# Eight plain float32 heads, three low-v splits on VectorE, and constants set up earlier in an attention and expert kernel

## The chip, the core and the metric

The kernel runs on one core of a Trainium2 chip. A core has TensorE (PE, with its weight loads shown as PEld), VectorE (DVE), ScalarE (ACT), GpSimd (POOL) and SyncE (SP), which issues most DMAs. The metric is the device time of one execution in microseconds (us), as a median of several runs.

## What is computed

Causal attention over 4 batches of 12 heads (448 positions, 64 columns per head), whose output is the input of a mixture of 8 experts: each of the 1792 positions goes to its best expert.

```
scores = scale * np.matmul(q, k.transpose(0, 1, 3, 2))     # masked above the diagonal
attn = exp(scores - max); attn = attn / (attn.sum(-1) + 1e-09)
x = attn @ v                                               # to [1792, 768]
logits = x @ w_gate + modality_bias[modality_id]
e_idx = argmax(logits);  gate_w = softmax(logits)[e_idx]
out[mask_e] = gate_w * (relu(x[mask_e] @ w1[e]) @ w2[e])   # for each expert e
```

## The kernel before

Products in full float32 take two passes of TensorE, each slow. So the kernel cuts most operands in a high part (rounded to the format fp32r) and a low part (the rest), and adds up products of parts in single passes. `hl` holds such parts of a pair of heads, `vhl` those of v for a group of four heads, `ph` and `pl` those of the transposed probabilities.

The attention stage is a loop of 48 iterations, `iteration(n)`, one per head, written out in software-pipeline order: TensorE in iteration n makes the scores of head n (`st_scores`, L270), transposes the probabilities of head n-2 (`st_trans`, L302), multiplies those of head n-3 with v (`st_pv`, L334 and L341, into the one bank `ot`), and from iteration 7 on joins heads and forms logits (`st_comb`, L394). VectorE takes the score maxima (L280, with accumulator reads), forms `pl` (L321), adds high and low halves of the output to `ut` (`st_out`, L365, which frees `ot`), and normalizes (L412, L422). ScalarE does the exponentials (L290), `ph` (L320) and the copy `hol` (L359).

GpSimd prepares operands ahead. For a pair m of heads, `split_qk(m)` (L194, L195) cuts query and key in iteration 2m-4, SP's `stack_qk(m)` (L211, L212) copies the parts into `st` in iteration 2m-3, and `split_kl(m)` (L200 the low key, L202 the zero-padded queries `qz`) follows there. For a group, `load_v`, `split_vh` (L242) and `split_vl` (L247) make `vhl`, of which there are two buffers. GpSimd also does every fourth normalization, parts of the routing (`route`), scatters (L501) and, at the end of attention, splits of the first expert's weights (`w1_chunk`, L675, L676).

The first pairs of heads skip all that: `first_load(m)` brings them in and `st_scores` multiplies them as plain float32 (`qh is None`). Before, these are the pairs 0 to 2, heads 0 to 5. The queries stand zero-padded in pieces of the raw buffers `raw1`, given by `first_view`.

Work that belongs to no head is put at an iteration with `later(n, f)`, `before(n, f)` or `soon(n, f)`, and `run_todo` runs it there: `setup_0`, `setup_1` and `setup_4` make constants, index tables and the modality bias, `shift_slots` (six pieces) makes slot constants, `after_batch` spreads the routing of a batch. The order of each engine's line is the order of this code; nothing is moved afterwards, and an engine waits at an instruction whose operands are not there.

After the loop the last heads are finished beside the first products of the experts (`pre_g1(t, ks)`: weight blocks ks of token block t), then comes the routing of the last batch (`choose`, `places` with products L476 to L482 on TensorE), then the experts.

Of the kernel before, what the change touches and what calls it, by code (L numbers as in the profile page):

```python
# [8 lines left out]
F32 = mybir.dt.float32  # L9
# [4 lines left out]
ALU = mybir.AluOpType  # L14
# [7 lines left out]
def attention_moe(  # L22
# [12 lines left out]
    V = nc.vector  # L35
    P = nc.gpsimd
    A = nc.scalar
    B, HP, _, _, S = qk.shape
# [3 lines left out]
    E, _, DF = w1.shape  # L42
# [3 lines left out]
    GH = 4  # L46
# [121 lines left out]
    def stack_view(t):  # L168
        return t[:, 0:2 * S].rearrange("p (c s) -> p c s", c=2)
# [15 lines left out]

    def load_qk(m):
        b, j = divmod(m, H // 2)
        raw[m] = t = stack_view(raw1[(5, 3, 4)[m % 3]])
        nc.sync.dma_start(out=t, in_=qk[b, j])

    def split_qk(m):
# [27 lines left out]
        stk.append([t[:, a] for a in range(2)])  # L219

    def first_view(m, c):
        k, j = (((3, 0), (3, 1), (4, 0)), ((2, 0), (2, 1), (4, 1)), ((0, 0), (0, 1), (1, 0)))[m][c]
        return raw1[k][:, j * S:(j + 1) * S]

    def first_load(m):
# [6 lines left out]
    def load_v(gr):  # L232
        b, u = divmod(gr, NG)
        c = slice(u * GH * D, (u + 1) * GH * D)
        nc.sync.dma_start(out=vraw[:, 0:3, :], in_=v[b, 0:384, c].rearrange("(t p) c -> p t c", p=128))
        nc.sync.dma_start(out=vraw[0:64, 3, :], in_=v[b, 384:448, c])
# [3 lines left out]
    def split_vh(gr):  # L240
        t = T([128, NTL, GH, 2, D], F32R, "vhl", 2)
        P.tensor_scalar(out=t[:, :, :, 0], in0=vsrc, scalar1=1.0, scalar2=0.0, op0=ALU.mult, op1=ALU.add)  # L242
        vhl[gr] = t

    def split_vl(gr):
        t = vhl[gr]
        P.tensor_tensor(out=t[:, :, :, 1], in0=vsrc, in1=t[:, :, :, 0].bitcast(F32), op=ALU.subtract)  # L247

    SPOS = [(0, 448), (1, 0), (1, 192), (0, 0)]
    ORD = (3, 0, 1, 2)  # L250
# [295 lines left out]
    def shift_slots(s, j):  # L546
        a = by_shift[s]
        if j == 0:
            ts(a[:, 0:1], tcol, 1.0, -float(s))
            ts(a[:, 1:2], tcol, 0.0, float(PZ - s))  # L550
            ts(a[:, 2:3], a[:, 0:1], float(2 * BLK), 0.0)
            ts(a[:, 3:4], a[:, 0:1], float(HB), 0.0)
        else:
            x = sm([128, 1], "slot")
            ts(x, a[:, 0:1], *((128.0, 128.0 * (PZ - s)) if j == 1 else (64.0, 192.0 * (PZ - s) + 128.0)))
            P.tensor_scalar(out=a[:, 2:3], in0=a[:, 2:3], scalar1=x, scalar2=0.0, op0=ALU.min, op1=ALU.add)
            if s and j == 2:
                P.tensor_tensor(out=a, in0=a, in1=by_shift[0], op=ALU.subtract)
# [318 lines left out]
    with tc.manual_schedule():  # L877
# [1 line left out]
            first_load(m)  # L879
        load_v(0)  # L880
        first_load(2)
        load_qk(3)
        nc.sync.dma_start(out=modi, in_=mod)
        nc.sync.dma_start(
            out=bias_sb.rearrange("p m o e -> p (m o e)"),
# [2 lines left out]

        V.memset(ones, 1.0)
        warm_bank = bank("x")  # L890
        for _ in range(24):
            nc.tensor.matmul(warm_bank[:, 0:128], lhsT=ones, rhs=ones, start=True, stop=True)
        warm = sm([1, 1], "warm")
        V.memset(warm, 0.0)
# [17 lines left out]
        for s in range(3):  # L912
            eng = P if s else V
            eng.memset(praw[s][0], 0.0)
            eng.memset(praw[s][1][:, 192:256], 0.0)
            eng.memset(praw[s][2][:, 320:384], 0.0)
            eng.memset(praw[s][3][:, 448:512], 0.0)
        wg = w_gate.rearrange("(j a p) e -> a p j e", a=2, p=64)
        for a in range(2):
            r = slice(a * 64, a * 64 + 64)  # L920
# [32 lines left out]
        def later(n, f):  # L953
            todo.setdefault(n, []).append(f)
# [9 lines left out]
                f()  # L964

        for j in range(2):
            later(3 + j, lambda j=j: V.memset(xg[j], 0.0))
            later(1 + j, lambda j=j: V.memset(sls[j][64:128, 0, E:E + 1], 1.0e6))
            later(1 + j, lambda j=j: V.memset(lts[j][64:128, 0], 0.0))

# [23 lines left out]

        later(0, setup_0)
        later(1, setup_1)
        later(2, lambda: V.memset(e8v[64:128, 0], 0.0))

        def setup_4():
            P.iota(ent[:, :, 0, 0], pattern=[[S, B]], base=0, channel_multiplier=1)  # L1000
# [55 lines left out]
        def pre_g1(t, ks):  # L1056
            if t not in g1b:
                g1b[t] = two_banks() if t else [bank("sa"), bank("sb")]
            for k in ks:
                for half in range(2):  # L1060
                    g1(t, half, g1b[t][half], [k])
# [12 lines left out]

        for k in range(KA):
            later(NHEAD - KA + k, lambda k=k: w1_chunk(k, P))
        later(4, setup_4)
        for s in range(2):
            for j in range(3):
                later(6 + 3 * s + j, lambda s=s, j=j: shift_slots(s, j))  # L1080

        def iteration(n):
            if n % 2 == 1 and 5 < n + 3 < NHEAD:
                stack_qk((n + 3) // 2)
            if n == 1:
                load_v(1)
            if n and n % GH == 0 and n // GH + 1 < B * NG:
                load_v(n // GH + 1)
            gr, i = divmod(n - 2 * GH, GH)
            comb = 0 <= gr < B * NG  # L1090
            if 0 <= n - 4 < NHEAD:
                st_out(n - 4)
            if comb:
                st_move(gr, i)
                st_norm(gr, i)
                b, u = divmod(gr, NG)
                if u == NG - 1:
                    later(n + 1, lambda i=i: x_store(b, i))
                    if i == NTL - 1:
                        after_batch(b, n)  # L1100
            run_todo((n,))
            if n in (2, 3):
                st_trans(n - 2)
            if n < NHEAD:
                st_scores(n)
            run_todo(n)
            if n == 0:
                split_vh(0)
                split_vl(0)
            if n % 2 == 1 and 5 < n + 3 < NHEAD:  # L1110
                split_kl((n + 3) // 2)
            if n % 2 == 0 and 5 < n + 4 < NHEAD:
                split_qk((n + 4) // 2)
            if n % GH == 1 and n > GH:
                st_sums(n // GH - 1, P)
            if n % GH == RECAT and n > GH:
                st_rec(n // GH - 1)
            if 0 <= n - 1 < NHEAD:
                st_exp(n - 1)
            if 0 <= n - 2 < NHEAD:  # L1120
                if n > 3:
                    st_trans(n - 2)
                run_todo(-n)
                st_split(n - 2)
            if 0 <= n - 3 < NHEAD:
                st_pv(n - 3)
                st_low(n - 3)
            gr, i = divmod(n - 2 * GH + 1, GH)
            if 0 <= gr < B * NG:
                st_comb(gr, i)  # L1130
            if n % GH == 2 and n // GH + 1 < B * NG:
                split_vh(n // GH + 1)
                split_vl(n // GH + 1)
            if n in (1, 3):
                load_qk(4 + n // 2)
            if n % 2 == 0 and n > 3 and n + 8 < NHEAD:
                load_qk((n + 8) // 2)

        for n in range(NHEAD):
            iteration(n)  # L1140
# [111 lines left out]
        for _, f in choose:  # L1252
            f()
        pre_g1(0, (3, 4))
        places()
        pre_g1(1, (0, 1, 2, 3))
        for i in range(2):
# [7 lines left out]
        sc_ = schedule_a(counts(B - 1))  # L1265
        for i in range(NTL):
            x_store(B - 1, i)
        pre_g1(0, (5,))
        ha, hb = (relu(o, i) for i, o in enumerate(g1b[0]))
        w2_chunk(2)  # L1270
        pre_g1(1, (4,))
# [154 lines left out]
```

## Time and profile before

| | |
|---|---|
| time, median of 3 runs | 499.09 us (496.9 to 499.83) |
| profiled execution: whole run, span of the trace | 498.88 us, 496.8 us |
| mean granted clock of TensorE, as a share of 2.4 GHz | 0.987 |
| busy: TensorE, VectorE, ScalarE, GpSimd | 470.7, 290.3, 276.4, 245.8 us |
| instructions | 10248 |

How to read it: an engine's row has the start in the span, the duration, the engine and line (of the kernel before), operation, out<-in, shapes and a count. In brackets stands the idle time of that engine just before, and after the arrow what ended it. Adjacent durations on an engine overlap a little, since instructions are pipelined; the distance from start to start is the cost. "x2" on a float32 product are its two passes.

### The profile page before, as it was taken

The numbers are of one execution on the slowest core, as the hardware profiler recorded it, in microseconds if no ns is written. First come the engines' busy times: TensorE is split into PE (matmuls) and PEld (weight loads), VectorE is DVE, ScalarE is ACT, GpSimd is POOL, SyncE is SP. The second block draws the span as 40 slices with busy tenths as digits, with TensorE's granted clock in tenths as the row PEclk, the third lists the DMA queues.
The fourth block names the chain that finished last, engine by engine and source line by source line (L and its number), as shares of the span: only waits on it lengthen the run. The fifth ranks groups of instructions, "written<-read, shape, count | busy, mean of one in ns | idle before, by whom it ended". The sixth has DMA issues, their size and how long they took to land. (4 is left out here: it accounts for less than half of the span.)

```text
span 496.8 us, 10248 instructions
## 1 busy us (share of the span) xinstructions
PE 470.7 (95%) x3307; PEld 443.0 (89%) x3307; DVE 290.3 (58%) x858; ACT 276.4 (56%) x680; POOL 245.8 (49%) x332
## 2 busy tenths in 40 slices
PE   8999899999899979989999999999999999999990
PEld 6799899999798979869999999999999999889770
DVE  4899899999889988987422017431120120283490
ACT  5799899999788978326212116612220211383670
POOL 8999999999999999942301104102001001021131
PEclk9999999999899999989999999999999999999997
DMA  7797799998987889491596204853001001076200
GB/s 189 199 257 214 183 236 251 281 237 206 292 214 182 188 182 327 126 202 3 163 381 208 81 1 144 292 203 98 34 1 53 33 2 63 33 279 194 104 13 7
DMA packets 43816, 78.91 MB, mean 159 GB/s; under 512 B 15582, under 2 KB 27614, under 8 KB 43744
## 3 DMA queue, kind: packets, MB, share of 16 engines
q1 hardware_dynamic: 40624, 66.94, 49.2%
q0 software_dynamic: 3040, 11.03, 6.6%
q8 instruction: 28, 0.46, 0.5%
q14 instruction: 44, 0.36, 0.3%
q10 hardware_dynamic: 80, 0.11, 0.1%
HBM read 48.10 MB, written 11.89 MB: 121 GB/s over the span
## 5 line engine op out<-in xcount | busy, mean ns | idle before, releaser
L732 POOL DMA_INDIRECT xg<-xs,idg x18 | 21.0, 1164 | 156.6 <-DVEq L1336 80.8
L290 ACT ACTIVATE p<-p,nm 128x448 f32<-128x448 f32 x192 | 94.8, 498 | 2.5 <-DVE nm L280 2.5
L770 DVE SCALAR_TENSOR_TENSOR htl<-g,hth 128x256 fp32r<-128x256 f32 x40 | 16.7, 425 | 104.6 <-ACT hth L769 104.6
L751 PE MATMUL g<-xh,w1h 128*128 128x256 f32 x240 | 67.1, 280 | 0.4 <-DVE htl L770 0.4
L753 PE MATMUL g<-xh,w1l 128*128 128x256 f32 x240 | 67.3, 280 | 0.0
L752 PE MATMUL g<-xl,w1h 128*128 128x256 f32 x240 | 67.0, 279 | 0.0
L321 DVE TENSOR_TENSOR pl<-pt,ph 128x1024 fp32r<-128x1024 f32 x48 | 58.3, 1215 | 7.6 <-ACT ph L320 7.2
L302 PE MATMUL pt<-ident,p 128*128 128x128 f32 x480 | 60.2, 273 | 0.0
L302 PEld LDWEIGHTS pt<-ident,p 128*128 128x128 f32 x480 | 55.3, 141 | 1.1
L334 PE MATMUL ot<-ph,vhl 128*128 128x448 f32 x192 | 50.5, 303 | 5.9 <-DVE ut L365 5.9
L320 ACT ACTIVATE ph<-pt 128x1024 fp32r<-128x1024 f32 x48 | 49.1, 1023 | 7.4 <-PE pt L302 6.3
L769 ACT ACTIVATE hth<-g 128x256 fp32r<-128x256 f32 x40 | 15.1, 383 | 63.5 <-PE g L753 63.5
L751 PEld LDWEIGHTS g<-xh,w1h 128*128 128x128 f32 x240 | 44.9, 187 | 0.6 <-DVE htl L770 0.6
L811 POOL DMA_INDIRECT out_dram<-row,idg x14 | 16.2, 1157 | 59.1 <-ACTq L1320 33.5
L752 PEld LDWEIGHTS g<-xl,w1h 128*128 128x128 f32 x240 | 45.2, 188 | 0.0
L753 PEld LDWEIGHTS g<-xh,w1l 128*128 128x128 f32 x240 | 45.1, 188 | 0.0
L334 PEld LDWEIGHTS ot<-ph,vhl 128*128 128x128 f32 x192 | 33.2, 192 | 7.9 <-DVE ut L365 6.4
L280 DVE CUSTOM_DVE_ANT_0 p<-sa,mask 128x448 f32<-128x448 f32 x96 | 36.2, 412 | 5.2 <-PE sa L270 4.9
L290 ACT ACTIVATION_READ_ACCUMULATOR p<-p,nm 128x1 f32 x192 | 36.5, 190 | 0.0
L280 DVE CUSTOM_DVE_ANT_0 p<-sb,mask 128x192 f32<-128x192 f32 x96 | 36.3, 411 | 0.0
L341 PE MATMUL ot<-pl,vhl 128*64 128x64 f32 x192 | 35.1, 298 | 0.7 <-DVE pl L321 0.7
L359 ACT ACTIVATE hol<-ot 64x448 f32<-64x448 f32 x48 | 26.0, 542 | 13.3 <-PE ot L334 10.8
(365 smaller groups left out, 1307.6 us busy)
## 6 DMA issues: line engine op xcount, KB each, us to landing
st<-hl SPq DMA_DIRECT2D x56, 224.0 KB
raw<-in_moe_w_dram SPq DMA_DIRECT2D x24, 512.0 KB
raw<-in_qk_dram SPq DMA_DIRECT2D x21, 448.0 KB
raw<-in_moe_w_dram SPq DMA_DIRECT2D x20, 384.0 KB
vraw<-in_v_dram SPq DMA_DIRECT2D x12, 384.0 KB
xs<-row SPq DMA_DIRECT2D x9, 384.0 KB
w1h<-hl SPq DMA_DIRECT2D x14, 224.0 KB
w1l<-hl SPq DMA_DIRECT2D x14, 224.0 KB
```

The lines of the kernel that those rows point to most:

```text
L280: V.tensor_tensor_reduce(out=z, in0=o, in1=m, scale=-scale, scalar=3.0e38, op0=ALU.add, op1=ALU.min, accum_out=nm[:n, i:i + 1],)
L290: A.activation(out=z, in_=z, func=AF.Exp, bias=nm[:n, i:i + 1], scale=-1.0, accum_out=sums[:n, b, i, h:h + 1],)
L302: nc.tensor.transpose(out=o, in_=a, identity=i)
L320: A.activation(out=ph, in_=t, func=AF.Copy)
L321: V.tensor_tensor(out=pl, in0=t, in1=ph.bitcast(F32), op=ALU.subtract)
L334: nc.tensor.matmul(o[:, q0:S], lhsT=t[:rows, kt, h].rearrange("p a d -> p (a d)"), rhs=ph[:rows, c0:c1], start=(n == 0), stop=(n == 1),)
L341: nc.tensor.matmul(o[0:D, q0:S], lhsT=t[:rows, kt, h, 0], rhs=pl[:rows, c0:c1], start=False, stop=False)
L359: A.activation(out=t, in_=ov[g][64:128, :S], func=AF.Copy)
L732: P.indirect_dma_start(out=xg[u][:n], out_offset=None, in_=xs[0:rows, :], in_offset=bass.IndirectOffsetOnAxis(ap=g[:n, 0:1], axis=0), boun ...
L751: nc.tensor.matmul(o, lhsT=ah, rhs=bh, start=first, stop=False)
L752: nc.tensor.matmul(o, lhsT=ah, rhs=bl, start=False, stop=False)
L753: nc.tensor.matmul(o, lhsT=al, rhs=bh, start=False, stop=last)
```

## The change

Pair 3 (heads 6 and 7) joins the plain pairs. Low v of the groups 0, 1 and 2 is made by VectorE, at the end of iterations 1, 4 and 6; of later groups by GpSimd as before, but two iterations after high v, and the load of the next v follows it. High v of group 1 moves from iteration 2 to 4. `setup_4` and `shift_slots` go to iterations 1 and 2, two memsets of `xg` to 0 and 2, that of `e8v` to 3. There are 32 warm-up products instead of 24. The key-query loads of the first split pairs use other raw buffers and iterations. After attention, `pre_g1(0, (5,))` stands before `places()`.

```diff
-        raw[m] = t = stack_view(raw1[(5, 3, 4)[m % 3]])
+        raw[m] = t = stack_view(raw1[(3, 4, 0)[m - 4] if m < 7 else (5, 3, 4)[(m - 7) % 3]])
...
-        k, j = (((3, 0), (3, 1), (4, 0)), ((2, 0), (2, 1), (4, 1)), ((0, 0), (0, 1), (1, 0)))[m][c]
+        k, j = (
+            ((3, 0), (3, 1), (4, 0)), ((2, 0), (2, 1), (4, 1)),
+            ((0, 0), (0, 1), (1, 0)), ((5, 0), (5, 1), (1, 1)),
+        )[m][c]
...
-    def split_vl(gr):
+    def split_vl(gr, eng):
         t = vhl[gr]
-        P.tensor_tensor(out=t[:, :, :, 1], in0=vsrc, in1=t[:, :, :, 0].bitcast(F32), op=ALU.subtract)
+        eng.tensor_tensor(out=t[:, :, :, 1], in0=vsrc, in1=t[:, :, :, 0].bitcast(F32), op=ALU.subtract)
...
-        load_qk(3)
+        first_load(3)
...
-        for _ in range(24):
+        for _ in range(32):
...
+        for a in range(2):
+            V.memset(first_view(3, a)[64 - a * 64:128 - a * 64], 0.0)
...
-            later(3 + j, lambda j=j: V.memset(xg[j], 0.0))
+            later(2 * j, lambda j=j: V.memset(xg[j], 0.0))
...
-        later(2, lambda: V.memset(e8v[64:128, 0], 0.0))
+        later(3, lambda: V.memset(e8v[64:128, 0], 0.0))
...
-        later(4, setup_4)
+        later(1, setup_4)
...
-                later(6 + 3 * s + j, lambda s=s, j=j: shift_slots(s, j))
+                later(2, lambda s=s, j=j: shift_slots(s, j))
...
-            if n % 2 == 1 and 5 < n + 3 < NHEAD:
+            if n % 2 == 1 and 7 < n + 3 < NHEAD:
                 stack_qk((n + 3) // 2)
-            if n == 1:
-                load_v(1)
-            if n and n % GH == 0 and n // GH + 1 < B * NG:
-                load_v(n // GH + 1)
...
-                split_vl(0)
-            if n % 2 == 1 and 5 < n + 3 < NHEAD:
+            if n % 2 == 1 and 7 < n + 3 < NHEAD:
                 split_kl((n + 3) // 2)
-            if n % 2 == 0 and 5 < n + 4 < NHEAD:
+            if n % 2 == 0 and 7 < n + 4 < NHEAD:
                 split_qk((n + 4) // 2)
...
-            if n % GH == 2 and n // GH + 1 < B * NG:
-                split_vh(n // GH + 1)
-                split_vl(n // GH + 1)
-            if n in (1, 3):
+            if n in (4, 6) or n % GH == 2 and n > 2 * GH and n // GH + 1 < B * NG:
+                split_vh(n // GH + 1 if n != 4 else 1)
+            if n in (1, 4, 6):
+                split_vl(n // 3, V)
+            if n % GH == 0 and n > 2 * GH:
+                split_vl(n // GH, P)
+            if n in (1, 3, 5, 7):
                 load_qk(4 + n // 2)
-            if n % 2 == 0 and n > 3 and n + 8 < NHEAD:
+            if n % 2 == 0 and n > 7 and n + 8 < NHEAD:
                 load_qk((n + 8) // 2)
+            if n in (1, 4) or n % GH == 1 and n > 2 * GH and n // GH + 1 < B * NG:
+                load_v(n // GH + 1 if n != 4 else 2)
...
         pre_g1(0, (3, 4))
+        pre_g1(0, (5,))
         places()
...
-        pre_g1(0, (5,))
```

On GpSimd, in the kernel before, the constants of iteration 1 end with `ebneg`, and the splits follow at once: of pair 3 (`hl`), of v of group 1 (high L242, low L247), the low key and the padded queries (here in `xh` and `w1h`), then the constants of iteration 4.

```order
L972 TENSOR_SCALAR ebneg<-ebase 128x8
L194 TENSOR_SCALAR hl<-raw_121 128x896
L195 TENSOR_TENSOR hl<-raw_121,hl 128x448
L242 TENSOR_SCALAR vhl<-vraw 128x16x64
L247 TENSOR_TENSOR vhl<-vraw,vhl 128x16x64
L200 TENSOR_TENSOR xh<-raw_121,hl 128x448
L202 TENSOR_SCALAR w1h_147<-raw_121,half 128x448 x2
L1000 IOTA ent 128x4
```

In the changed kernel the constants of iterations 1 and 2 stand there in one block, which ends with the slot constants `by_shift`, and the first splits are those of pair 4 in iteration 4.

```order
L977 TENSOR_SCALAR ebneg<-ebase 128x8
L1005 IOTA ent 128x4
...
L561 TENSOR_TENSOR by_shift_99<-by_shift_99,by_shift_98 128x4
L194 TENSOR_SCALAR hl<-raw_119 128x896
L195 TENSOR_TENSOR hl<-raw_119,hl 128x448
L245 TENSOR_SCALAR vhl<-vraw 128x16x64
L200 TENSOR_TENSOR xl<-raw_119,hl 128x448
L202 TENSOR_SCALAR qz_154<-raw_119,half 128x448 x2
L375 TENSOR_SCALAR rec<-sums 128x16
```

High v of group 1 (L242, now L245) has moved behind the constants of two iterations, its low part is gone from this line, and the low key follows high v directly.

On VectorE, at the passage from iteration 4 to 5, the kernel before has the `xg` memset and `pl` of head 2, then `ut` of head 1 and the score maxima of head 5.

```order
L967 MEMSET xg_129 128x768
L321 TENSOR_TENSOR pl<-pt,ph 128x1024
L365 TENSOR_TENSOR ut_132<-ot,hol_135 64x448
L280 ISA p_3_167,nm<-sa,mask 128x448
L280 ISA nm 128x1
```

The changed kernel has low v of group 1 at that place.

```order
L324 TENSOR_TENSOR pl<-pt,ph 128x1024
L250 TENSOR_TENSOR vhl<-vraw,vhl 128x16x64
L368 TENSOR_TENSOR ut_132<-ot,hol_135 64x448
L283 ISA p_3_167,nm<-sa,mask 128x448
L283 ISA nm 128x1
```

Between `pl` and `ut` VectorE now has a subtraction that reads what GpSimd has written; the memset is gone from here.

On TensorE, ahead of the routing products of the last batch (`x<-pc,onesf`), the kernel before ends with weight block 4 of the first token block (banks `sa` and `sb`).

```order
L753 MATMUL sa<-w1h_3197,xl 128x512
L751 MATMUL sb<-w1h_3197,xh 128x512
L752 MATMUL sb<-w1l_3198,xh 128x512
L753 MATMUL sb<-w1h_3197,xl 128x512
L476 MATMUL x<-pc,onesf 128x40
```

The changed kernel puts the six products of block 5 between.

```order
L756 MATMUL sb<-w1h_3191,xl 128x512
L754 MATMUL sa<-w1h_3193,xh 128x512
L755 MATMUL sa<-w1l_3194,xh 128x512
L756 MATMUL sa<-w1h_3193,xl 128x512
L754 MATMUL sb<-w1h_3193,xh 128x512
L755 MATMUL sb<-w1l_3194,xh 128x512
L756 MATMUL sb<-w1h_3193,xl 128x512
L479 MATMUL x<-pc,onesf 128x40
```

The routing products and all that follows them stand six products later in TensorE's line, in which the six have only changed places.

## Rows read from the trace of the kernel before

**Rows 1.** Windows: busy us (instructions) of PE, PEld, DVE, ACT, POOL, then PEclk, DMA.

```profile
35.00:190.00 155.00, 146.88 (x1181) 141.34 (x1180) 143.78 (x485) 140.57 (x400) 146.53 (x190) 0.99 0.89 223
...
225.00:465.00 240.00, 239.43 (x1618) 232.35 (x1618) 72.00 (x153) 76.28 (x143) 32.98 (x29) 1.00 0.36 122
...
132.00:136.00 4.00, 3.85 (x18) 3.67 (x19) 3.97 (x15) 1.79 (x7) 3.63 (x7) 0.57 1.05 371
...
215.00:220.00 5.00, 5.00 (x18) 4.00 (x17) 4.55 (x23) 0.00 (x0) 0.22 (x1) 0.73 1.02 136
```

**Rows 2.** Waits of TensorE, 0 to 225 us: us in total, times, longest.

```profile
PE ot L334 <- DVE ut L365: 5.9, 6, 2.1
PE x L476 <- DVE row L422: 1.6, 1, 1.6
PE sa L270 <- POOL qz L202: 1.6, 1, 1.6
PE sa L270 <- DMA st<-hl: 1.5, 2, 0.8
...
PE ot L341 <- DVE pl L321: 0.7, 1, 0.7
```

**Rows 3.** Timeline of TensorE: the start, iterations 4 to 8, two waits.

```profile
1.12 2.74 PE L892 MATMUL x<-ones 128*128 128x128 bf16 x24 [1.12 <-DVE warm L894]
...
4.23 1.83 PE L270 MATMUL sa<-raw,raw 128*128 128x448 f32 x2 [0.37 <-DVE half L911]
...
21.48 0.92 PE L270 MATMUL sa<-raw,raw 128*128 128x448 f32 x2
...
24.33 0.54 PE L334 MATMUL ot<-ph,vhl 128*128 128x448 f32 x2
...
25.41 0.37 PE L270 MATMUL sa<-w1h 128*128 128x448 f32 x1
...
28.64 0.36 PE L270 MATMUL sa<-w1l 128*128 128x448 f32 x1
...
33.08 0.44 PE L270 MATMUL sa<-st 128*128 128x448 f32 x1
...
85.30 0.56 PE L334 MATMUL ot<-ph,vhl 128*128 128x448 f32 x2 [0.52 <-DVE ut L365]
...
132.16 0.74 PE L334 MATMUL ot<-ph,vhl 128*128 128x448 f32 x2 [2.11 <-DVE ut L365]
```

**Rows 4.** Timeline of GpSimd: constants and splits, and one weight split.

```profile
10.89 2.36 POOL L247 TENSOR_TENSOR vhl<-vraw,vhl 128x1024 fp32r<-128x1024 f32 x1
...
15.81 0.94 POOL L194 TENSOR_SCALAR hl<-raw 128x896 fp32r<-128x896 f32 x1
...
17.95 1.05 POOL L242 TENSOR_SCALAR vhl<-vraw 128x1024 fp32r<-128x1024 f32 x1
...
23.77 0.14 POOL L1000 IOTA ent<- 128x4 int32 x1
...
26.42 0.94 POOL L194 TENSOR_SCALAR hl<-raw 128x896 fp32r<-128x896 f32 x1
...
37.79 0.19 POOL L544 TENSOR_SCALAR slot<-by_shift 128x1 f32<-128x1 f32 x1
...
38.37 1.15 POOL L200 TENSOR_TENSOR xh<-raw,hl 128x448 fp32r<-128x448 f32 x1
...
205.89 2.38 POOL L676 TENSOR_TENSOR w1l<-raw,w1h 128x1024 fp32r<-128x1024 f32 x1
```

**Rows 5.** Timeline of VectorE: a memset, the logits of batch 1, a weight split.

```profile
21.80 0.70 DVE L967 MEMSET xg<- 128x768 f32 x1
...
129.18 0.93 DVE L454 TENSOR_REDUCE lg<-ltp 128x32 f32<-128x416 f32 x1 [1.58 <-POOL ltp L412]
...
206.83 2.26 DVE L679 TENSOR_TENSOR w2l<-raw,w2h 128x768 fp32r<-128x768 f32 x1
```

**Rows 6.** Line L679 of VectorE: subtractions of 128x1024; ns minimum/median/maximum, first and last start.

```profile
L679 DVE TENSOR_TENSOR w1l<-raw,w1h x19: 1216/1220/1307, 203.0 to 473.4; 128x1024 fp32r<-128x1024 f32 x19
```

## The prediction

> **What bounds the kernel now.** The reading starts with the busy time by stage [rows 1]. In the attention stage (35 to 190 us) four engines are almost equally full: TensorE 146.9 of 155 us, GpSimd 146.5, VectorE 143.8. In the expert stage (225 to 465 us) TensorE is busy 239.4 of 240 us. So whatever TensorE saves before 225 us moves the end by the same amount, and only its idle time and its clock before that point can be won.
>
> Next come TensorE's waits up to 225 us [rows 2]: 5.9 us in six waits for `ut` (the copy that frees the one bank `ot`), 1.6 for `qz`, 1.5 for the DMA of `st`, 1.6 for the routing of the last batch, 0.7 for the first `pl`. Behind most of them stands GpSimd. It works without a gap, late against its place in the program: the query and low-key pieces for heads 10 and 11 belong to iteration 7, which TensorE begins at 28.64 [rows 3], and GpSimd begins them at 38.37 [rows 4], 9.7 us later. At 129.18 VectorE waits 1.58 us for a GpSimd row of logits, and TensorE then stands 2.11 us at 132.16 and runs at a mean granted clock of 0.57 from 132 to 136, mostly its lower level (1.2 of 2.4 GHz) [rows 1, 3, 5]. At 85.30 the same routing work, without a wait for GpSimd, costs 0.52 us [rows 3].
>
> **The change part by part.** All sums are in time of the profiled execution: span 496.8, whole run 498.88, practically the median of 499.09.
>
> *Warm-up.* Eight more warm products at 2.74/24 = 0.114 us each make 0.9 us, the first ending at 3.86 now; scores start at 4.23 [rows 3]. TensorE is occupied until 4.77, so at most 0.54 is lost if the clock rises no earlier; less if it does. I take +0.2 (ends −0.4 and +0.54).
>
> *Constants earlier.* The `e8v` memset no longer stands before the first `pl` of VectorE, whose wait cost TensorE 0.7 [rows 2]. In its place stand one `xg` memset (0.70 [rows 5]) and, an iteration before, the first split of low v, both of which fit into time in which VectorE waits for scores. I take −0.55 (ends 0 and −0.7).
>
> *Heads 6 and 7 as plain products.* A plain head's iteration takes 25.41 − 21.48 = 3.93 us, the next, split one 28.64 − 25.41 = 3.23 [rows 3]. Two heads: +1.4.
>
> *GpSimd's work.* One pair of splits goes, and three low-v splits of 2.36 us [rows 4]. Low v on VectorE is a subtraction of 128x1024 from SBUF; the same form elsewhere has a median of 1.22 us [rows 6].
>
> *Where VectorE now waits.* The subtraction for group 1 stands in VectorE's line in iteration 4, behind `pl` and ahead of `ut`, and needs high v from GpSimd. GpSimd's line up to there: setup_1 from the end of low v, 10.89 + 2.36, to 15.81 = 2.6; setup_4 23.77 to 26.42 = 2.65; six slot pieces, 0.58 for one (37.79 to 38.37), longer for the two that open a chain: 4.0, estimated from that row; the split of a pair 15.81 to 17.95 = 2.1; high v 1.05 [rows 4]. Begun at 10.9, where the moved low v stood, that ends at 23.4. VectorE is there at about 22.1: in iteration 4 it ran an `xg` memset from 21.80 for 0.70 [rows 5] and then `pl` (a form like the 1.22 us one), to about 23.6; without that memset and the one of iteration 3 it is there some 1.4 us earlier. So it stands 1.3 us and goes on at 23.4; behind it are `ut` and, behind that, the score reads. With 1.22 for the subtraction and 0.6 for `ut` (448 columns, estimated as half of it) the bank comes free at 25.3, where TensorE could begin the products with v at 23.7 (24.33 before [rows 3], less the 0.6 of above). That is a hold of 1.55.
>
> *Two readers of SBUF.* At 206.83 a VectorE subtraction of only 768 columns with both inputs in SBUF takes 2.26 us, longer than the median 1.22 of 1024 columns, while GpSimd subtracts from 205.89 for 2.38 [rows 4 to 6]: it seems to have waited that instruction out. After high v GpSimd goes straight on to a 1.15 us subtraction (as at 38.37 [rows 4]). If that starts first, VectorE's low v waits up to 1.15. I take half, 0.6, since who starts first is open; the hold becomes 2.15. The Trainium skill (SBUF — State Buffer, section Who interferes with whom) says that a VectorE instruction with two SBUF inputs and a GpSimd instruction that reads SBUF shut each other out, the first holding the port to its end. This trace agrees at 206.83; by the rule the sum is the second rival's or, if VectorE starts first, 0.6 us better per split.
>
> The same happens in iteration 6: high v waits for head 3's products (two buffers), and low v follows; there VectorE is ready just then, so only the shut-out of 0.6 is added (ends 0 and 1.15). A hold of 2.15 is like the 2.11 after which the clock fell (3.85 busy us at 0.57: 1.65 lost [rows 1]); after the 1.6 for `qz` no such fall shows. I take half, 0.8 (ends 0 and 1.65). Small idle times in iterations 4 to 8 disappear in these holds: iteration 7 took 33.08 − 28.64 = 4.44 [rows 3], 1.2 more than the 3.23 of its like, and the first product that joins the heads explains about half; with a little of iteration 4 I take −0.75 (ends 0 and −1.2).
>
> Cost at the start: 0.2 − 0.55 + 1.4 + 2.15 + 0.6 + 0.8 − 0.75 = 3.85. The ends go from 0.3 (no shut-out, half the hold, no clock loss) to 5.75.
>
> *What GpSimd's lead gives back.* It is freed of 4.5 + 3 × 2.36 = 11.6 us and idles perhaps 4 of them (high v can't run ahead of head products); also, from group 3 on the logits row stands before low v, 2.4 us earlier in its line. So the lateness of 8 to 10 us in the attention stage should become 2 to 6. Then go: the wait for `qz`, 1.6; of the 2.11 at 132.16 what exceeds 0.52, 1.59; the clock loss behind it, 1.65; the waits for `st`, 1.5, whose DMAs follow GpSimd's split; of the other 3.3 us for `ut` [rows 2] I count 0.7, for the next batch's meeting of the same kind. Sum 7.0. VectorE's own routing work stays in the path and is late next: the remaining 3.1 us of `ut` are not counted. Ends: 1.6 (`qz` alone) and 8.
>
> *The tail.* Six products for column block 5 now stand ahead of the routing products, where TensorE waits 1.6 us. GpSimd ends the weights of that block about 3 us earlier and TensorE arrives some 3 us earlier; the routing itself, behind GpSimd's last logits, comes 3 us earlier too. So the wait shrinks by about half: −0.7 (ends 0 and −1.4). From 215 to 220 the granted clock is 0.73, 1.35 us lost in 5 [rows 1]; a wait of 0.9 is less than those after which it fell: −1.35 (ends 0 and −1.35).
>
> Sum: 498.88 + 3.85 − 7.0 − 2.05 = 493.7 us.
>
> **The rivals.**
> 1. *Shut out for good.* GpSimd starts first both times and the clock falls: the start costs 5.75 in place of 3.85, and the time is 495.6. For it: the 2.26 us row, and that GpSimd's next instruction needs nothing. (The Trainium skill's rule above is this case.) Against: the median of 1.22 lies at the low end, so most of these were not shut out.
> 2. *The lead is eaten.* Loads of v now stand a group's quarter later, behind low v; if high v waits for them in every group, GpSimd is as late at 130 us as before, and the change doesn't do what it seems made for. Only `qz` and the tail are won: 498.88 + 3.85 − 1.6 − 2.05 = 499.1. For it: GpSimd is at 146.5 of 155 us, with hardly 1 us to spare per group, and two batches bring scatters. Against: logits before low v, whatever the lead.
> 3. *VectorE's line holds every later head.* Low v of group 1 waits in VectorE's order for GpSimd, `ut` waits behind it, TensorE for `ut`, and GpSimd's next high v for TensorE; VectorE, 143.8 of 155 us busy, can't win it back. Each us by which GpSimd's high v of group 1 ends after 23.4 is one us of the time. The gains are gone when it ends 5.2 us late, and it is slower by 0.5% from about 7 us, the clock's other 0.85 included; with 9 us the time is 503.5. It could come from the key pair or v behind the four table fills in SP's queue, needed at 20 us. Against: in the trace before, v issued at 13.3 was there at 17.95 without a wait [rows 4].
>
> **How the numbers follow.** The forecast 493.7, own range 490 to 496.5: 0.53. Rival 1, 495.6: 0.15. Rival 2, 499.1: 0.20. Rival 3, 503.5: 0.12. Before is 499.09; a measurement can tell about 0.5%, 2.5 us, from no change. Forecast and rival 1 are faster by more: 0.68. Rival 2 is the same: 0.20. Rival 3 is slower: 0.12. The range takes in the cheap start (490, and the larger tail: 488) and rival 2 with its uncertainty: 488 to 501.5; rival 3 is left out.
>
> **What would show it.** After: no wait of TensorE for `qz`; VectorE's low v in iterations 4 and 6 begins after 22 us behind an idle of about 1.3 and lasts 1.2 (not shut out) or above 2; the score product of head 8 starts some 4 us later than 33.08; VectorE's logits reduction near 130 us has no wait for GpSimd and no clock below 1 follows; the product before the last routing is block 5. The forecast is wrong if TensorE's later waits stay though GpSimd is early, or if the start is dearer than 6 us.

## The result and the profile after

The changed kernel takes 502.19 us (median of 19 runs, 499.65 to 506.78), the kernel before 498.19 (19 runs, 496.82 to 501.1) beside it on the same chips. The ratio is 1.0085, 95% interval 1.0065 to 1.0106: slower by 0.85%, some 4.2 us, where 493.7 was forecast; the time lies above the stated range of 488 to 501.5. A ratio in this document is taken from the runs of both kernels beside each other, is not the quotient of their medians, and leaves out runs more than 1.5% above the fastest of their kernel (one each in experiments 1, 3 and 4). The profiled run took 502.35 us, close to the median, with a span of 500.5 (before: 498.88 and 496.8).

Where it went is read from the starts of the same products in both traces:

| TensorE's product | before | after | after is late by |
|---|---|---|---|
| scores of head 0 | 4.23 | 4.51 | 0.28 |
| scores of head 5 | 21.48 | 21.20 | −0.28 |
| scores of head 9 | 36.69 | 42.70 | 6.01 |
| scores of head 15 | 60.44 | 64.58 | 4.14 |
| scores of head 33 | 127.62 | 131.80 | 4.18 |
| scores of head 34 | 134.76 | 136.27 | 1.51 |
| scores of head 38 | 150.44 | 152.20 | 1.76 |
| scores of head 39 | 155.52 | 159.82 | 4.30 |
| scores of head 47 | 188.69 | 191.84 | 3.15 |
| `oh` (chosen experts as ones and zeros) of the routing before the last | 191.86 | 196.10 | 4.24 |
| first transpose of `hol` | 223.70 | 225.00 | 1.30 |
| last product | 485.22 | 488.79 | 3.57 |

Six microseconds are lost in iterations 5 to 8, 4.5 come back at two places, 2.5 are lost again at head 39, 1.1 come back and go again between there and 196, 2.9 come back around the last routing, and 2.3 of these are lost by the end.

Two more traces, of experiments further down, hold the same code up to the last routing: experiment 2 that of the kernel before, experiment 1 that of the changed kernel. They show how much of the table belongs to one run:

| us between starts of TensorE's products | before | experiment 2 | after | experiment 1 |
|---|---|---|---|---|
| head 0 to head 5 | 17.25 | 16.65 | 16.69 | 15.58 |
| head 5 to head 9 | 15.21 | 14.85 | 21.50 | 20.91 |
| head 9 to `oh` of the routing before the last | 155.17 | 158.75 | 153.40 | 153.56 |

The loss in iterations 5 to 8 is in every pair, 5.7 to 6.7 us. What comes back from head 9 to `oh` is 1.8 against the first trace of the kernel before and 5.4 against the second.

TensorE's waits up to 230 us; they answer to [rows 2]. Columns as there.

```profile
PE ot L337 <- DVE ut L368: 8.7, 8, 2.4
PE x L483 <- POOL oh L473: 1.5, 1, 1.5
PE ot L756 <- DVE htl L785: 1.3, 1, 1.3
...
PE sa L273 <- DMA st<-hl: 1.0, 1, 1.0
```

The wait for `qz` is gone, and so are those of 1.6 for the last routing and 0.7 for the first `pl`. But `ut` costs 8.7 in place of 5.9. TensorE's timeline shows where (start, duration; in brackets the idle time before):

```profile
21.20 0.91 PE L273 MATMUL sa<-raw,raw 128*128 128x448 f32 x2
...
26.63 0.56 PE L337 MATMUL ot<-ph,vhl 128*128 128x448 f32 x2 [2.34 <-DVE ut L368]
...
28.15 1.70 PE L273 MATMUL sa<-raw,raw 128*128 128x448 f32 x2
...
33.31 0.91 PE L273 MATMUL sa<-raw,raw 128*128 128x448 f32 x2
...
37.60 0.53 PE L337 MATMUL ot<-ph,vhl 128*128 128x448 f32 x2 [1.20 <-DVE ut L368]
...
39.06 0.46 PE L273 MATMUL sa<-st 128*128 128x448 f32 x1
...
134.77 0.56 PE L337 MATMUL ot<-ph,vhl 128*128 128x448 f32 x2 [0.54 <-DVE ut L368]
...
157.05 0.90 PE L337 MATMUL ot<-ph,vhl 128*128 128x448 f32 x2 [2.42 <-DVE ut L368]
...
196.10 0.18 PE L483 MATMUL x<-oh,upper 128*128 128x32 bf16 x1 [1.51 <-POOL oh L473]
...
217.46 0.38 PE L479 MATMUL x<-pc,onesf 1*128 1x40 f32 x2 [0.24 <-DVE row L425]
...
229.09 0.45 PE L756 MATMUL ot<-w2h,htl 128*128 128x384 f32 x1 [1.31 <-DVE htl L785]
...
238.97 0.18 PE L648 MATMUL g<-ad,ones 32*128 32x32 bf16 x1 [0.76 <-DVE own L642]
```

Against [rows 3]: iteration 5 takes 6.95 us in place of 3.93, iteration 6 5.16 in place of 3.23, iteration 7 5.75 in place of 4.44. At 28.15 the score product takes 1.70 where the same one at 33.31 takes 0.91: the clock. At 134.77 the wait is 0.54 where it was 2.11, and 157.05 is a new wait of 2.42. The windows (as in [rows 1]) give the clock, and the expert stage:

```profile
26.00:31.00 5.00, 4.37 (x16) 3.40 (x17) 3.88 (x12) 2.50 (x9) 3.32 (x5) 0.66 0.73 186
...
155.00:160.00 5.00, 2.95 (x13) 2.86 (x14) 4.96 (x17) 1.23 (x2) 4.33 (x7) 0.69 0.96 225
...
215.00:225.00 10.00, 9.76 (x48) 7.55 (x47) 8.51 (x42) 2.87 (x6) 4.62 (x7) 1.00 1.03 184
225.00:465.00 240.00, 237.35 (x1601) 230.37 (x1600) 74.45 (x167) 75.19 (x140) 34.84 (x31) 1.00 0.37 125
```

Behind the holds at 26.63 and 157.05 the mean clock is 0.66 and 0.69, a mixture of its two levels, 1.2 and 2.4 GHz; around the last routing it is now 1.00. Now the two engines that TensorE waits for. First VectorE:

```profile
11.35 1.31 DVE L250 TENSOR_TENSOR vhl<-vraw,vhl 128x1024 fp32r<-128x1024 f32 x1
...
23.77 2.15 DVE L250 TENSOR_TENSOR vhl<-vraw,vhl 128x1024 fp32r<-128x1024 f32 x1 [1.10 <-POOL vhl L245]
...
34.70 2.10 DVE L250 TENSOR_TENSOR vhl<-vraw,vhl 128x1024 fp32r<-128x1024 f32 x1
...
153.24 2.10 DVE L529 SCALAR_TENSOR_TENSOR ft<-cnt,fm,e 128x8 f32<-128x8 f32 x1
155.26 1.21 DVE L324 TENSOR_TENSOR pl<-pt,ph 128x1024 fp32r<-128x1024 f32 x1
156.39 0.61 DVE L368 TENSOR_TENSOR ut<-ot,hol 64x448 f32<-64x448 f32 x1
...
214.43 1.00 DVE L457 TENSOR_REDUCE lg<-ltp 128x32 f32<-128x416 f32 x1
...
228.35 0.68 DVE L785 TENSOR_TENSOR htl<-g,hth 128x512 fp32r<-128x512 f32 x1
...
234.29 0.69 DVE L785 TENSOR_TENSOR htl<-sa,hth 128x512 fp32r<-128x512 f32 x1 [2.05 <-ACT hth L784]
```

And GpSimd, which answers to [rows 4]:

```profile
11.84 0.89 POOL L977 TENSOR_SCALAR e<-evals 128x32 f32<-128x32 f32 x1
...
22.68 1.06 POOL L245 TENSOR_SCALAR vhl<-vraw 128x1024 fp32r<-128x1024 f32 x1
23.70 1.15 POOL L200 TENSOR_TENSOR xl<-raw,hl 128x448 fp32r<-128x448 f32 x1
...
33.56 1.04 POOL L245 TENSOR_SCALAR vhl<-vraw 128x1024 fp32r<-128x1024 f32 x1 [3.98 <-PE ot L337]
34.57 1.16 POOL L200 TENSOR_TENSOR xh<-raw,hl 128x448 fp32r<-128x448 f32 x1
...
50.59 1.04 POOL L245 TENSOR_SCALAR vhl<-vraw 128x1024 fp32r<-128x1024 f32 x1 [5.08 <-DMA vraw<-in_v_dram]
...
152.95 2.36 POOL L250 TENSOR_TENSOR vhl<-vraw,vhl 128x1024 fp32r<-128x1024 f32 x1
...
186.47 2.37 POOL L250 TENSOR_TENSOR vhl<-vraw,vhl 128x1024 fp32r<-128x1024 f32 x1
```

Read the pairs. VectorE's low v at 23.77 lies beside GpSimd's subtraction of 23.70 to 24.85 and ends 1.07 after it; the one at 34.70 lies beside 34.57 to 35.73 and ends 1.07 after it. Each was kept out until the other was done. At 153.24 an instruction of 8 columns takes 2.10 us and ends with GpSimd's low v, at 155.3; `pl` and `ut` stand behind it, and TensorE behind `ut`. At 11.84 it is the other way round: a GpSimd instruction of 32 columns takes 0.89 and ends at 12.7, as VectorE's low v of 11.35 does. The Trainium skill (SBUF — State Buffer, section Who interferes with whom) says that the order of issue, not the shape, decides who is blocked; these rows agree.

GpSimd, for which the trace before shows no idle time from 9.8 to 91 us, idles 3.98 and 5.08 us. What it was freed of, it mostly waited away.

### The profile page after: what moved, and what is told of

Its sections match the earlier page's. It is cut to its first block, busy times and chain, and to the rows that moved or that the text cites. A ratio compares the mean times of both kernels' runs of the same rounds, so it can differ in the third digit from the quotient of the medians.

```text
span 500.5 us, 10267 instructions
## 1 busy us (share of the span) xinstructions
PE 472.8 (94%) x3315; PEld 444.0 (89%) x3315; DVE 298.1 (60%) x863; ACT 276.2 (55%) x680; POOL 235.7 (47%) x324
## 4 chain that ended last, share of the span: by engine, by line
PE 50%; POOL 15%; DVE 14%; DMA 10%; issue 5%; ACT 2%; SPq 1%; POOLq 0%; DVEq 0%; ACTq 0%
PE g L756 7%; PE g L754 7%; PE g L755 7%; DMA vraw<-in_v_dram 5%; DVE p L283 3%; POOL vhl L250 2%; DVE pl L324 2%; DMA raw<-in_moe_w_dram 2%; DMA table<-ent,si 2%; PE ot L754 2%; PE x L756 2%; PE ot L755 2%; PE ot L756 2%; PE x L755 2%; PE x L754 2%
```

## The experiments

The spread of single runs is wide (7 us for the changed kernel), and each program has one trace. The changed kernel's and that of experiment 1 differ by 1.7 us at head 8, and 1.1 of that comes from head 0, whose first score product takes 1.81 us in the one and 0.97 in the other. So effects are read from rows, not from one span against another.

**1. Block 5 back behind the routing.**

```diff
         pre_g1(0, (3, 4))
-        pre_g1(0, (5,))
         places()
...
             x_store(B - 1, i)
+        pre_g1(0, (5,))
```

> The changed kernel, only with the six products of column block 5 back behind the last routing, where the kernel before has them. Theory A (VectorE's gapless routing and schedule chain, 213.9 to 238.7 us, sets the end, so that what TensorE won ahead of 225 us it gave back in waits of 1.31 and 0.76 for VectorE): TensorE stands about 1.6 us at the routing again and the clock falls behind it, its shift at 225 us against the kernel before grows from 1.3 to about 4, but the waits for htl and own vanish and the time is that of the changed kernel to within 0.8 us (500.5 to 501.3 of span). Theory B (TensorE's own work sets the end, the two later waits are accidents): 1.4 + 1.5 = 2.9 us slower than the changed kernel, span 503.4.

Measured: 500.99 us, ratio to before 1.0054 (1.0027 to 1.0080), not slower than the changed kernel's 1.0085 (1.0065 to 1.0106); theory B's 2.9 us more would be 1.014. Its waits of TensorE from 200 to 240 us:

```profile
PE x L479 <- DVE row L425: 1.6, 1, 1.6
PE ot L337 <- DVE ut L368: 0.7, 1, 0.7
```

The wait of 1.6 is back, and those for `htl` (the low part of the experts' transposed hidden values) and `own` (a step of the schedule) are gone. Two parts of theory A's forecast fail: behind this wait the granted clock stays at 1.00 (215 to 220 us), and the first transpose of `hol` is 1.15 us later than before, not 4. Its core stands: the time does not hang on where the six products are. From VectorE's last reduction of logits to the start of its first `htl` it is 14.13 us here, 13.92 with block 5 ahead (214.43 to 228.35), 14.77 before. These are the rows before:

```profile
210.19 1.00 DVE L454 TENSOR_REDUCE lg<-ltp 128x32 f32<-128x416 f32 x1
...
223.85 0.96 DVE L679 TENSOR_TENSOR w2l<-raw,w2h 128x768 fp32r<-128x768 f32 x1 [0.50 <-ACT w2h L678]
...
224.96 0.69 DVE L782 TENSOR_TENSOR htl<-g,hth 128x512 fp32r<-128x512 f32 x1 [0.15 <-ACT hth L781]
```

Just ahead of `htl` VectorE idles 0.65 us there; in the changed kernel that idle time is gone. So TensorE could come some 0.65 us earlier and no more: beyond that it waits for `htl`. Further on VectorE is not the bound alone, since at 234.29 it idles 2.05 us itself for `hth`, which ScalarE makes from TensorE's transposes.

**2. The kernel before, with block 5 ahead.** The same move the other way round, alone.

> The kernel before, only with the six products of column block 5 ahead of the last routing. Theory A (VectorE's chain of 23.7 to 24.9 us from the last logits to the schedule sets the end): TensorE's wait at the routing falls from 1.61 to about 0.3 and the clock stays up behind it, but it then waits 1 to 2 us for htl or own, and the time is that of the kernel before, within 0.8 us. Theory B (the prediction's step: the products fill TensorE's wait and save the clock): 2.05 us faster, up to 2.75.

Measured: 497.43 us, ratio 0.9995 (0.9972 to 1.0019). Its waits of TensorE from 200 to 240 us:

```profile
PE ot L753 <- DVE htl L782: 1.5, 1, 1.5
PE ot L334 <- DVE ut L365: 0.7, 1, 0.7
PE ot L752 <- DVE w2l L679: 0.2, 1, 0.2
```

The wait at the routing is gone (1.61 before), and 1.5 stand at `htl` in its place. Theory A again; the prediction's −2.05 lies outside the interval (−1.4 to +0.9 us).

Up to the last routing this is the code of the kernel before, and the trace differs from the first one where the prediction built on it. There is no wait for the first `pl`, and at 129 us VectorE does not wait for GpSimd's row of logits; TensorE's wait behind that is 0.75, and the granted clock is 1.00 from 132 to 136 us, where it was 0.57. Instead the wait for `qz` is longer, with a clock of 0.79 from 54 to 62 us.

```profile
56.44 0.47 PE L270 MATMUL sa<-xl,qz 128*128 128x448 f32 x1 [1.96 <-POOL qz L202]
...
131.92 0.56 PE L334 MATMUL ot<-ph,vhl 128*128 128x448 f32 x2 [0.75 <-DVE ut L365]
```

**3. Low v of groups 1 and 2 back on GpSimd.**

```diff
             if n in (1, 4, 6):
-                split_vl(n // 3, V)
+                split_vl(n // 3, V if n == 1 else P)
```

> The changed kernel, only with low v of groups 1 and 2 back on GpSimd (2.4 us each, behind high v, in iterations 4 and 6). Theory A (the start costs 6.0 us at head 9 because these two subtractions stand ahead of ut in VectorE's line, wait for GpSimd's high v and are shut out by its next subtraction, and the clock falls behind the hold): the holds of 2.34 and 1.20 and the clock's 1.8 go, the shift of head 9 against the kernel before falls from 6.0 to 1 to 1.5, GpSimd's added 4.8 us fit into its idle 3.98 and 5.08, and the time is some 4 us under the changed kernel (span 496 to 497). Theory B (the price of the start is the two plain float32 heads, the constants and the longer warm-up): the shift of head 9 stays above 4 and the span above 499.

Measured: 500.03 us, ratio 1.0052 (1.0022 to 1.0081). The start behaves as theory A says: no hold in iterations 5 and 7, iterations 5, 6 and 7 take 3.93, 3.92 and 4.41 us, and head 9 starts at 35.74, 0.95 ahead of before (0.89 of it stand at head 1 already). But the time does not follow: the interval overlaps the changed kernel's. VectorE waits twice for GpSimd's tie work (`eq`, which settles which expert a token takes where logits are equal):

```profile
89.43 0.19 DVE L468 TENSOR_REDUCE m<-eq 128x4 f32<-128x36 f32 x1 [1.60 <-POOL eq L465]
...
139.76 0.19 DVE L468 TENSOR_REDUCE m<-eq 128x4 f32<-128x36 f32 x1 [2.85 <-POOL eq L465]
```

In GpSimd's line the low v of 2.39 and 2.38 us (86.03, 136.40) stands just ahead of that tie work, and head 36 starts 3.36 us later than before. Theory A's "fits into its idle time" is wrong: GpSimd still idles 5.44 us ahead of group 3's v.

```profile
49.98 1.04 POOL L245 TENSOR_SCALAR vhl<-vraw 128x1024 fp32r<-128x1024 f32 x1 [5.44 <-DVE nm L283]
```

The row names VectorE's `nm`, which ends at that moment, but TensorE's products of head 7, which free the buffer, end at 42.8 already; what is left to wait for is the load of that v, issued at 41.1.

**4. The constants back in iterations 4 and 6 to 11.**

```diff
-        later(1, setup_4)
+        later(4, setup_4)
...
-                later(2, lambda s=s, j=j: shift_slots(s, j))
+                later(6 + 3 * s + j, lambda s=s, j=j: shift_slots(s, j))
```

> The changed kernel, only with the two blocks of GpSimd constants back in iterations 4 and 6 to 11. High v of group 1 is then done some 6 us earlier (near 17 to 18 us), GpSimd stands for head 3's products when VectorE does low v of group 1. Theory A (wait plus shut-out): that low v takes about 1.3 us, starts without a wait near 22.7, and TensorE's hold in iteration 5 falls from 2.34 to under 0.6 without a clock loss; in iteration 6 the shut-out (2.1 us) stays; the shift of head 9 falls from 6.0 to about 2.5. Theory B (VectorE is simply too full in these iterations for a subtraction of 1.2 us): the hold of iteration 5 stays above 1.5 and the shift above 4. The later part may differ by about 1 us either way, since the slot pieces return to GpSimd's full stretch.

Measured: 500.2 us (494.58 to 504.17), ratio 1.0018 (0.9985 to 1.0050), clear of the changed kernel's: some 3.3 us of its 4.2 are gone. VectorE's low v of groups 1 and 2:

```profile
22.39 1.22 DVE L250 TENSOR_TENSOR vhl<-vraw,vhl 128x1024 fp32r<-128x1024 f32 x1
...
30.74 1.22 DVE L250 TENSOR_TENSOR vhl<-vraw,vhl 128x1024 fp32r<-128x1024 f32 x1
```

The same two instructions take 1.22 in place of 2.15 and 2.10, without a wait: GpSimd ends high v of group 1 at 19.1 and is past the subtraction behind it at 20.3, before VectorE comes. In iteration 6 VectorE comes first, and GpSimd's one-column instruction of 30.88 takes 1.25 us and ends at 32.1, VectorE's at 32.0. TensorE waits 0.23 and 0.33, and head 9 is 1.18 late in place of 6.01. Theory A, and VectorE is not too full for 1.2 us. That iteration 6 is free as well I had not expected. The profiled run took 504.17 us, 4 us above the median, so nothing is read from its later part.

**5. GpSimd's low v of group 9 one iteration later.**

```diff
-            if n % GH == 0 and n > 2 * GH:
+            if n % GH == 0 and n > 2 * GH and n != 36 or n == 37:
                 split_vl(n // GH, P)
```

> The changed kernel, only with GpSimd's low v of group 9 (152.95 us there) one iteration later in its line. Theory A (VectorE's instruction of 8 columns with two SBUF inputs took 2.10 us at 153.24 because GpSimd's low v held the port to 155.31): it now meets a GpSimd subtraction of 1.15 us at most and ends by about 154.3, TensorE's wait of 2.42 at 157.05 falls to about 1.2, and with the clock staying high 1.2 to 2.5 us are won at head 39. Theory B (the stall came from the chain of ScalarE and VectorE itself): the stall stays above 2 and head 39 starts where it did, 159.8.

Measured: 500.47 us, ratio 1.0046 (1.0027 to 1.0065), an interval that only touches the changed kernel's. In place of 2.42 at 157.05 TensorE waits 0.26 and 0.76, and iteration 38 takes 5.18 us in place of 7.62; before it took 5.08. So theory A: the stall hung on 8 columns. Its price is less sure. Experiment 1's trace has the same code with the same stall (2.06 us, and TensorE waits 1.92 at 156.10), but its clock stays at 1.00 and iteration 38 takes 5.89: 0.8 us more than before, where the changed kernel's takes 2.5 more. VectorE now meets that same low v two instructions later, with three columns:

```profile
153.37 1.17 DVE L533 SCALAR_TENSOR_TENSOR sch<-sch_a,xf,sch_b 1x3 int32<-1x3 f32 x1
```

**6. GpSimd's low v and the loads of v one iteration earlier, groups 3 to 11.**

```diff
-            if n % GH == 0 and n > 2 * GH:
-                split_vl(n // GH, P)
+            if n % GH == 3 and 2 * GH < n < NHEAD - 1:
+                split_vl((n + 1) // GH, P)
...
-            if n in (1, 4) or n % GH == 1 and n > 2 * GH and n // GH + 1 < B * NG:
+            if n in (1, 4) or n % GH == 0 and n > GH and n // GH + 1 < B * NG:
                 load_v(n // GH + 1 if n != 4 else 2)
```

> The changed kernel, only with GpSimd's low v of groups 3 to 11 one iteration earlier (iteration 3 of a group in place of 0) and the next load of v, which has to follow it, one iteration earlier too. Theory A (GpSimd's lead is eaten by the loads of v: it idles 5.08 us at 45.5 for group 3's and 0.5 to 1.6 in later groups, and is as late as before at 130 us for that): these idles fall to under 1 us together, GpSimd's logits row and its tie work come 3 to 5 us earlier in the middle, so that TensorE's waits for ut at the routing of the first three batches (0.65, 0.54, 2.42) fall by half and its wait for oh at 196 (1.51) vanishes: 2 to 4 us under the changed kernel. Theory B (GpSimd is held by TensorE, whose products free its buffers, and lateness is set by the order inside the group): the idles move to other waits and the time stays within 1 us of the changed kernel.

Measured: 501.41 us, ratio 1.0051 (1.0021 to 1.0082); the interval overlaps the changed kernel's, so a gain is likely but not shown. The wait for `oh` vanishes and that at 157 falls to 1.27, as theory A says; but the scores of head 46 now wait 2.41, where they waited 1.00. Theory A's first number fails:

```profile
49.86 1.05 POOL L245 TENSOR_SCALAR vhl<-vraw 128x1024 fp32r<-128x1024 f32 x1 [4.68 <-DVE nm L283]
```

The load was issued at 36.9, 5.4 us earlier, yet high v begins only 0.7 us earlier. At 49.8 VectorE's `nm`, which the row names, ends, and so do TensorE's products of head 7, which free the buffer that high v of group 3 writes; the next two waits of this kind, at 64.43 and 78.99, name TensorE's products. So with TensorE 6 us late, GpSimd is held by TensorE, as theory B has it. In the changed kernel these products end at 49.8 too, and the load adds only the 0.8 us up to 50.59.

**7. Experiments 3 and 6 together.** Both diffs.

> The run with GpSimd's low v one iteration earlier, and low v of groups 1 and 2 on GpSimd as well. Theory A (the start costs what VectorE's line costs, the middle what the loads of v cost): the shift of head 9 against the kernel before is 0 to -1, the routing meetings at 84, 133 and 157 us cost no more than 0.7 each, TensorE does not wait for oh at 192, and the time is 494 to 496, under the kernel before. Theory B (GpSimd can't carry the two splits in the first 50 us): the middle loses 2 to 4 us as it did with low v on GpSimd alone, and the time is 498 to 500.

Measured: 496.6 us (493.8 to 500.9), ratio to before 0.9963 (0.9934 to 0.9992): 0.4% faster than the kernel before, faster than the changed one, and 0.6 us above theory A's 494 to 496. Head 9 starts at 36.54, 0.15 ahead of before, head 34 at 131.66, 3.10 ahead. TensorE's waits up to 230 us:

```profile
PE ot L337 <- DVE ut L368: 3.9, 6, 1.3
PE sa L273 <- DVE pl L324: 2.4, 1, 2.4
PE sa L273 <- DMA w1h<-hl: 1.6, 2, 1.3
PE ot L756 <- DVE htl L785: 1.4, 1, 1.4
```

No wait for `oh`, 3.9 for `ut` in place of 8.7, and the meetings at 85, 130 and 151 us cost 0.53, 0.51 and 1.27; theory A allowed 0.7 for each. The 2.4 in the list is head 46's, as in experiment 6. VectorE's waits of 1.60 and 2.85 for ties are gone, and GpSimd reaches high v of group 3 earlier:

```profile
47.34 1.05 POOL L245 TENSOR_SCALAR vhl<-vraw 128x1024 fp32r<-128x1024 f32 x1 [1.94 <-DVE rec L382]
```

GpSimd's idle time ahead of group 3's high v is 1.94. Each edit alone gave about a third of a per cent, together 1.2 (1.0085 to 0.9963): with low v on VectorE TensorE is late and holds GpSimd, without it the load does, and only when both go does GpSimd keep a lead. That this is why the two add up to more is read from the three traces at 45 to 50 us; no run tests it by itself.

## Why the prediction was wrong

**Plain heads: right; warm-up and `pl`: not shown.** Two plain heads with the idle time that they fill were to cost 1.4 − 0.75; in experiment 3, where nothing else disturbs, iterations 6 and 7 take 3.92 and 4.41 against 3.23 and 4.44: 0.66. The wait of 0.7 for `pl` is gone, but experiment 2's trace, the kernel before up there, has none either. Head 1 starts 0.45 us later than before in the changed kernel, and 0.5 to 1.0 earlier in four of the six experiments on it, beyond the lower end of −0.4.

**Where VectorE waits: right in place and mechanism.** High v was to end at 23.4, and ended at 23.7; the hold of TensorE was to be 2.15, and was 2.34. Experiments 3 and 4 take it away in two different ways. The hold ends when GpSimd and VectorE are done, whenever TensorE comes: in the traces of the changed kernel and of experiments 1, 5 and 6 TensorE arrives between 23.2 and 24.3 and goes on between 26.57 and 26.90.

**Two readers of SBUF: mis-sized.** Half a shut-out was taken twice; both were whole, because GpSimd's next subtraction starts 0.07 and 0.13 us before VectorE's low v. Iteration 6 cost TensorE 1.20, not 0.6, and the clock took about 2 (the 6.29 lost from head 5 to 9, less 0.66 and the two holds), not 0.8. The start was 3.85 in the sum and 6.01 in the trace, just over its upper end of 5.75: the place where rival 1 is right. Experiment 4 shows it in the time as well, 3.3 us. (The lower end of 0.3 does not follow from its own terms: half the hold, no shut-out and no clock loss make 1.1.)

**"What GpSimd's lead gives back": the step that failed.** It was −7.0; from head 9 to the product of `oh` at 196.10 it is 4.24 − 6.01 = −1.8, and −5.4 against experiment 2's trace. Of its named parts `qz` came, −1.87. At 132 the table shows −2.67 for the stall and the clock (1.59 + 1.65 forecast), but experiment 2, with the old code, has a wait of 0.75 and a clock of 1.00 there, so this gain is not shown to be the lead's. Of the 1.5 for `st` 1.00 is still there, at head 46. Three things in the step were wrong. The step let GpSimd idle 4 of its 11.6 us; it idled 3.98 and 5.08 in the first 50 us alone, and the lead was mostly gone (experiments 3 and 6 show by what it is held). It counted where low v leaves GpSimd's line, the logits, and not where it arrives: just ahead of the tie work, where it cost waits of 1.60 and 2.85 in experiment 3 (one of 0.67, at 139.40, in the changed kernel); and the last one, at 186.47, stands ahead of `oh` for 196.10, where TensorE waits 1.51 in place of 0.42. And it used the rule of two readers at two places only, those that the change makes on purpose, though the same rule covers each small VectorE instruction that meets the moved low v: 2.10 us for 8 columns at 153.24, 2.54 us of time at head 39 (0.8 in experiment 1's trace, where the clock stayed up). The forecast for that place was −0.7. Even experiment 7, where GpSimd keeps a lead and the start has no hold, is only 1.8 us under the kernel before.

**The tail: wrong.** −2.05 was forecast; from 196.10 to the last product it is 3.57 − 4.24 = −0.7, and in the times of experiments 1 and 2 the place of the six products makes no difference that shows. TensorE did win 2.94 up to 225 us, wait and clock as forecast, and lost 2.27 again. That the clock's 1.35 belonged to the wait is not shown: experiment 1 has the wait and a clock of 1.00. The step took TensorE's wait at the routing for the bound, because [rows 1] show TensorE full behind 225. Ahead of `htl` stands VectorE's line, which from the last logits on has 0.65 us of slack in the trace before and none in the changed kernel's (rows in experiment 1).

**The rivals.** Each holds a piece. Rival 1 is the start. (The sum by the rule of two readers, which the prediction calls the second rival's, is this one's, 495.6.) Rival 2 said that the lead is eaten, and it was, by loads only where TensorE is on time. Rival 3 had VectorE's line as the carrier, and 0.3 us of lateness of high v in place of the 7 that it asked for. The mistake was to treat them as one or the other: the forecast and each rival keep one term bad and the others good. The time is the sum of a bad start (+2.2 against the forecast), the lost lead (+5.2) and the empty tail (+1.4), 8.8, and 502.35 − 493.7 is 8.65. That is the split of the profiled pair; with experiment 2's trace as the kernel before, the start is worse by 3.2 and the lead by 1.7. All three terms were taken too well, but how much of the miss is whose stays open.

**The signs.** As promised: no wait for `qz`, low v in iteration 4 after 22 us behind an idle of 1.10, and above 2 long; logits near 130 us without a wait; block 5 ahead of the last routing. Not so: no idle ahead of VectorE's low v in iteration 6, head 8 six us late, not four. And one of the prediction's two signs of being wrong came, if barely: a start dearer than 6 us.

## What to carry to other kernels

When work moves between engines, read what it will stand ahead of in the line where it arrives, and what will run beside it there: here a long GpSimd instruction that reads SBUF held VectorE instructions with two SBUF inputs until it ended, even one of 8 columns, and all that queued behind them waited too. Before crediting a change with a wait that is gone, look whether a second trace of the old code has that wait. Freed time on an engine is a gain only as far as its buffers and loads let it run ahead, so find what holds it next before counting a lead. And where one engine waits near the end, check whether the engine that it waits for has slack behind that point before counting the wait as won.

## What the hardware showed that I had not expected

- The size of the blocked instruction didn't matter here: VectorE with 8, 3 and 32 columns took 2.10, 1.17 and 2.38 us beside GpSimd (the last in experiment 5, at 206.04, beside a weight split), while VectorE's `pl`, which reads one input from PSUM, takes 1.15 to 1.23 us all 48 times in every trace.
- The length of a hold doesn't say whether the clock falls: in iteration 5 it fell behind holds of 2.34 (changed kernel, 0.66 from 26 to 31 us) and 2.81 us (experiment 6, 0.66), and stayed at 1.00 behind 3.38 and 3.46 (experiments 1 and 5). At the last routing it fell behind 1.61 (before, 0.73 from 215 to 220 us) and stayed at 1.00 behind 1.64 (experiment 1). Why is open.
- With 32 warm products the first score product took about 1.8 us in three of the seven traces (changed kernel, experiments 4 and 6) and 0.97 to 1.12 in the others, which is worth about 1 us; with 24 it took 1.83 in both traces. So the longer warm-up wins in some runs, and costs 0.1 to 0.5 us (the start of head 1) in the others. The granted clock reads 1.00 from 0 to 8 us both in the changed kernel and in experiment 1, so the rows do not say what makes the product slow.
